# Pattern copies moved from three engines to SP's transfers, with new ranks, load order, gates and places of identity matmuls

## The chip, the cores and the metric

The kernel runs on one core of one Trainium2 chip. The metric is the device time of one execution in microseconds; three executions of the kernel before took 271.74, 271.98 and 272.30 us, the median is 271.98.

## What is computed

Inputs are q, k and v (4 batches, 8 heads, 768 tokens, 64 numbers, float32) and two weight matrices. Attention looks, for each query, only at the 6 best of 24 chunks of 32 keys; the chunks are ranked by an upper bound from each chunk's largest and smallest key. A feed-forward layer follows.

```python
k_min, k_max = k_chunks.min(axis=3), k_chunks.max(axis=3)          # per chunk of 32 keys
ub = sum(maximum(q * k_min, q * k_max))                             # per query and chunk
ub = where(causal, ub, -1e9); top = argsort(ub)[..., -6:]
scores = where(selected & causal, q @ k.T / sqrt(64), -1e9)
x = softmax(scores) @ v                                             # 3072 tokens x 512
h = x @ w_in                                                        # 512 -> 2048
out = (h * clip(h + 3, 0, 6) / 6) @ w_out                           # 2048 -> 512
```

## The kernel before

Two heads make a pair (16 pairs), two pairs with one half of the tokens (384) make a unit (16 units); a batch and a half make a group of the feed-forward layer (8 groups). Units 0 to 3 are batch 0, and they go another way than the rest: their K and Q are turned by TensorE (`turn`, KT and QT in PSUM), while batches 1 to 3 load K and Q in an order that VectorE's 32 by 32 transposes can turn (`load`, `turn_out`, KF and QF).

A unit goes through these steps: the limits of each chunk (`limits`, KMA, VectorE), the bounds (`bounds`, UBT, TensorE; for batches 1 to 3 two units at once), the selection (`bounds_in`, `largest`, `select`, `select_out`, VectorE, ending with the transposed mask MT), the scores (`scores`, SPS, TensorE), exponentials (PT, ScalarE), a triangle (`triangle`, POOL), the values (`values`, PVP, TensorE), and their division (`values_out`, Xb, VectorE). A group then turns its tokens (XTP to XT, or through DRAM as BT, BD, BF) and runs the layer: 16 tiles of HP (4 matmuls each), a relu on ScalarE (U), a multiply on VectorE (GT), and 48 or 64 matmuls of OP, whose sums go out through OT.

The mask enters the scores as further rows of the product: for batch 0 as a matmul with the constant pattern EB, for batches 1 to 3 as rows of K's own tile. K has six tiles (KL0 to KL5), each for the pairs p, p + 6, and so on; the two halves of EB that lie beside a pair's keys are copied into a tile once, before its first pair of batch 1 or later (`beside`, called by `masks_beside`): 12 copies of 64 partitions by 768 bfloat16, each on VectorE, ScalarE or POOL, whichever the planner finds first.

The order of all of this is set by a planner (`Plan`). Each step has an engine or a choice of engines, an estimated length, a rank, the steps that it needs, and the buffers that it takes and gives back. `order` goes through time: whenever an engine is free, the ready step of lowest rank for which there is room begins. The steps are then written out in that order, and every engine runs its own steps in that order, whatever the real times are. `SHIFT` adds a number to the ranks of single steps, found by a search. The planner also has estimates for transfers: `share` is the speed of a transfer of SP beside a transfer of weights.

SP issues nearly all transfers, in its order: first the loads of batch 0 (K, Q and V in `SEQ`), then those of batch 1, and so on. POOL issues the four halves of the weights (WIN and WOUT, two of 1 MB each); ahead of each, `load_weights` reads one number of a tile that must have landed (`GATE`, `seen`): before, the first half of WIN waits for a V load (V2), and each other half for the half before it.

TensorE's clock falls when it idles; so, in the first 45 us, where the planner sees it idle, matmuls with an identity matrix (IDENTB) fill the time. Before, `occupy` puts them behind a step, into 128 columns of its PSUM tile that are left over for this (`spare`).

PSUM has 4 banks for all tiles but the scores (`bank`, m in the plan), which are taken and given back in turn.

Of the kernel before, what the change touches and what calls it, by code (L numbers as in the profile page):

```python
# [45 lines left out]
}  # L46


class Plan:

# [118 lines left out]
def kernel(  # L169
# [188 lines left out]

    spare = []

    def occupy(times):
        for _ in range(times):
# [626 lines left out]
```

## Time and profile before

| | |
|---|---|
| median of three executions | 271.98 us |
| the profiled execution | 271.37 us |
| its span, from the first to the last instruction | 269.7 us |
| TensorE busy | 256.8 us (95%) |
| VectorE, ScalarE, POOL busy | 209.4, 191.6, 128.7 us |
| granted clock | at least 0.99 in each stretch |

Busy times are the sums of an engine's instructions that the profiler recorded. Each engine has a queue of its own and works in its order; a row of a timeline names in brackets for how long the engine had been idle, and which instruction of another engine, or which transfer (DMA), ended the wait. For a transfer the time from issue to landing is told apart from the time in which the issue itself stood in SP's queue.

### The profile page before, as it was taken

The numbers are of one execution on the slowest core, as the hardware profiler recorded it, in microseconds if no ns is written. First come the engines' busy times: TensorE is split into PE (matmuls) and PEld (weight loads), VectorE is DVE, ScalarE is ACT, GpSimd is POOL, SyncE is SP. The second block draws the span as 40 slices with busy tenths as digits, with TensorE's granted clock in tenths as the row PEclk, the third lists the DMA queues.
The fourth block names the chain that finished last, engine by engine and source line by source line (L and its number), as shares of the span: only waits on it lengthen the run. The fifth ranks groups of instructions, "written<-read, shape, count | busy, mean of one in ns | idle before, by whom it ended". The sixth has DMA issues, their size and how long they took to land.

```text
span 269.7 us, 6517 instructions
## 1 busy us (share of the span) xinstructions
PE 256.8 (95%) x2350; PEld 152.7 (57%) x2373; DVE 209.4 (78%) x588; ACT 191.6 (71%) x306; POOL 128.7 (48%) x289
## 2 busy tenths in 40 slices
PE   7997999898999999999999999999999999999994
PEld 4645565654445677644664566654665756555443
DVE  7799898989799997899989999999894424857000
ACT  3589899685527899765984499953998874868021
POOL 4168579533767485559734666752842310200000
PEclk9999999999999999999999999999999999999999
DMA  8999999999948999954995599114103003201122
GB/s 166 219 198 188 190 175 154 176 149 185 212 108 117 127 157 176 186 164 139 150 159 141 157 155 181 40 60 139 39 4 117 5 38 139 58 0 41 39 78 79
DMA packets 122720, 33.71 MB, mean 125 GB/s; under 512 B 113216, under 2 KB 118080, under 8 KB 122688
## 3 DMA queue, kind: packets, MB, share of 16 engines
q1 hardware_dynamic: 117952, 28.71, 62.2%
q0 software_dynamic: 3136, 4.19, 9.5%
q10 hardware_dynamic: 1600, 0.39, 0.7%
q8 instruction: 18, 0.29, 0.6%
q14 instruction: 14, 0.11, 0.2%
HBM read 29.23 MB, written 8.26 MB: 139 GB/s over the span
## 4 chain that ended last, share of the span: by engine, by line
PE 73%; DMA 10%; DVE 8%; SPq 4%; ACT 2%; issue 1%; ACTq 0%; DVEq 0%
PE OP L602 28%; PE HP L587 23%; PE SPS L497 9%; DMA KS<-in_k_dram 8%; PE PVP L530 6%; PE UBT L442 4%; SPq L229 2%; DVE GT L595 2%; PE SPS L494 2%; DMA VS<-in_v_dram 2%; ACT PT L507 1%; PE OP L610 1%; SPq L237 1%; DVE KMA L401 1%; DVE KMA L400 1%
## 5 line engine op out<-in xcount | busy, mean ns | idle before, releaser
L587 PE MATMUL HP<-XT,WIN 128*128 128x384 bf16 x512 | 92.4, 326 | 2.4 <-DVE GT L595 2.3
L507 ACT ACTIVATE PT<-SPS 128x1024 bf16<-128x1024 f32 (+1 forms) x96 | 85.3, 927 | 12.0 <-PE SPS L497 9.9
L602 PE MATMUL OP<-WOUT,GT 128*128 128x512 bf16 x345 | 82.3, 379 | 1.9 <-issue 0.5
L592 ACT ACTIVATE U<-HP,THREE 128x384 bf16<-128x384 f32 x128 | 73.0, 594 | 15.1 <-PE HP L587 8.8
L595 DVE SCALAR_TENSOR_TENSOR GT<-U,HP 128x384 bf16<-128x384 bf16 x128 | 67.2, 545 | 14.9 <-ACT U L592 11.0
L587 PEld LDWEIGHTS <-WIN 128*128 128x128 bf16 x512 | 48.5, 98 | 34.4 <-issue 4.0
L602 PEld LDWEIGHTS <-GT 128*128 128x128 bf16 x368 | 35.1, 98 | 40.2 <-issue 3.7
L512 POOL TENSOR_SCALAR_AFFINE_SELECT PT<-PT 128x256 bf16<-128x256 bf16 x96 | 38.9, 418 | 35.9 <-ACT PT L507 34.9
L497 PE MATMUL SPS<-QLA,KL 128*128 128x384 bf16 (+2 forms) x240 | 36.3, 278 | 0.0
L628 ACT ACTIVATE OT<-OP 128x512 f32<-128x512 f32 x22 | 13.1, 597 | 27.4 <-PE OP L602 27.0
L331 POOL TENSOR_SCALAR_AFFINE_SELECT KL<-KF 64x384 bf16<-64x384 f32 x48 | 23.9, 501 | 14.4 <-DVE KF L387 12.1
L331 POOL TENSOR_SCALAR_AFFINE_SELECT QLA<-QF 64x384 bf16<-64x384 f32 x48 | 24.6, 512 | 12.2 <-DVE QF L387 6.3
L497 PEld LDWEIGHTS <-KL 128*128 128x128 bf16 x240 | 21.7, 98 | 12.8 <-issue 0.6
L530 PEld LDWEIGHTS <-PT 128*128 128x128 bf16 x672 | 23.9, 97 | 3.1 <-issue 0.4
L530 PE MATMUL PVP<-VB,PT 128*128 128x65 bf16 x672 | 25.6, 194 | 0.0
L411 ACT ACTIVATE QR<-QF 128x384 f32<-128x384 f32 x30 | 15.4, 531 | 9.4 <-DVE QF L387 9.3
L542 DVE TENSOR_TENSOR Xb<-PVP,RINV 128x384 bf16<-128x384 f32 x32 | 18.5, 579 | 1.1
L580 POOL COPY XT<-BF 128x384 bf16<-128x384 bf16 x20 | 9.3, 504 | 16.7 <-DMA BF<-BD 16.6
L536 DVE RECIPROCAL RINV<-PVP 128x6 f32<-128x6 f32 x32 | 5.9, 185 | 12.6 <-PE PVP L530 12.2
L387 DVE STREAM_TRANSPOSE KF<-KS 128x384 f32<-128x384 f32 x24 | 13.2, 560 | 1.7 <-DMA KS<-in_k_dram 1.3
L387 DVE STREAM_TRANSPOSE QF<-QS 128x384 f32<-128x384 f32 x24 | 12.8, 555 | 2.0 <-DMA QS<-in_q_dram 2.0
L400 DVE TENSOR_REDUCE KMA<-KF 128x12 f32<-128x384 f32 x24 | 13.1, 545 | 0.4
(80 smaller groups left out, 235.8 us busy)
## 6 DMA issues: line engine op xcount, KB each, us to landing
out_dram<-OT SPq DMA_DIRECT2D x23, 256.0 KB, 2.3
KS<-in_k_dram SPq DMA_DIRECT2D x24, 192.0 KB, 5.5
QS<-in_q_dram SPq DMA_DIRECT2D x24, 192.0 KB, 6.5
VT<-in_v_dram SPq DMA_DIRECT2D x24, 192.0 KB, 4.5
WIN<-in_moe_w_in_dram POOLq DMA_DIRECT2D x2, 1024.0 KB, 9.4
WOUT<-in_moe_w_out_dram POOLq DMA_DIRECT2D x2, 1024.0 KB, 10.1
BD<-BT SPq DMA_DIRECT2D x5, 384.0 KB, 2.4
BF<-BD SPq DMA_DIRECT2D x20, 96.0 KB, 2.3
```

The source lines that it names most:

```text
L331: nc.gpsimd.affine_select(out=to, in_=x, pattern=[[0, n]], compare_op=A.is_ge, fill=0.0, base=0, channel_multiplier=0)
L387: nc.vector.transpose(T[:], st[name][:, st["i"], half * HC:(half + 1) * HC, :].rearrange("p c e -> p (c e)"))
L400: nc.vector.tensor_reduce(out=over, in_=chunks, axis=X_AXIS, op=A.max)
L497: nc.tensor.matmul(SP[:, j, c0:c0 + n], lhsT=KLS[st["pair"] % 6][:, j, jb * P:(jb + 1) * P], rhs=st["QL", half][:, j, at:at + n], start=Tr ...
L507: nc.scalar.activation(PT[:, :, 0:cols], SP[:, :, 0:cols], ACT.Exp, scale=scale)
L512: nc.gpsimd.affine_select(out=PT[:, :, c0:c0 + P], in_=PT[:, :, c0:c0 + P], pattern=[[0, 2], [1, P]], compare_op=A.is_ge, fill=0.0, base=0 ...
L530: nc.tensor.matmul(PVP[:, j, n, :], lhsT=PT[:, j, c0:c0 + P], rhs=st["VB"][:, jb, j, :], start=(jb == 0), stop=(jb == qb))
L542: nc.vector.tensor_tensor(out=to, in0=PVP[:, :, :, 0:D], in1=RINV[:].to_broadcast([P, 2, HB, D]), op=A.mult)
L587: nc.tensor.matmul(HP[:], lhsT=WIN[:, kt, f * P:(f + 1) * P], rhs=g["XT"][:, kt, :, :], start=(kt == 0), stop=(kt == KT_HID - 1))
L592: nc.scalar.activation(U[:], g["HP", f][:], ACT.Relu, bias=THREE[:], scale=1.0)
L595: nc.vector.scalar_tensor_tensor(out=g["GT"][:, f, :], in0=g["U", f][:], scalar=6.0, in1=g["HP", f][:], op0=A.min, op1=A.mult)
L602: nc.tensor.matmul(g["OP", t][:], lhsT=g["GT"][:, f, t * P:(t + 1) * P], rhs=WOUT[:, f, :], start=(f == 0), stop=(f == FT - 1))
```

## The change

- `beside` issues a transfer on SP from EB to K's tile in place of a copy; `masks_beside` plans it as a step of SP and a transfer. 12 copies leave VectorE, ScalarE and POOL, 12 issues come to SP.
- `GATE` reads other tiles: the first half of WIN waits for V1, the second for K4 (the first K load of batch 1), the first half of WOUT reads Q3, the second K1. POOL still issues them one after the other.
- The planner's estimates differ (`BEHIND`, `share` for each kind of transfer, weights 6.3 and 7.3 in place of 6.6 and 7.6), and a transfer under way at 15.3 us takes 1.35 us longer (`FETCH`, a packet of instructions).
- `SHIFT` is another table, so the order differs from the first us to the last; two lines of it are shown.
- Identity matmuls go ahead of a step, into the step's own tile (`occupied`), in steps for which the planner sees TensorE idle over 0.3 us, counted from when their bank came free.

```diff
 SHIFT = {
-    4: -885.8, 6: -49.2, 8: -980.9, 10: -841.2, 12: -1020.7, 14: -50.4, 16: -1.5, 18: -911.2, 20: 8.9, 22: -4.1, 28: -823.6, 30: -2.5, 32: -915.5, 40:
+    10: -869.7, 12: -1031.5, 14: -962.7, 16: -1673.7, 18: -1927.7, 20: -992.4, 22: 73.2, 28: -901.7, 36: 882.4, 38: 1034.2, 40: 956.6, 46: 1047, 52:
...
-    BEHIND = dict(PE=0.24, ACT=0.15, DVE=0.15, POOL=0.15, SP=0.3, DMA=0.9, GEN=0.0, WT=1.2)
+    BEHIND = dict(PE=0.24, ACT=0.15, DVE=0.15, POOL=0.15, SP=0.3, DMA=0.7, GEN=0.0, WT=1.2)
     COLD = 6.5
+    FETCH = 15.3, 1.35
...
+                        st["idle"] = now - max([free[e], *(opened.get((held[0], held[2]), 0.0) for held in st["take"])])
...
-                            length = min(length / 0.15, weights + max(length - 0.15 * weights, 0.0))
+                            length = min(length / st["share"], weights + max(length - st["share"] * weights, 0.0))
+                            if now <= self.FETCH[0] < now + length:
+                                length += self.FETCH[1]
...
+    def occupied(T):
+        for _ in range(idle.pop(0) if idle else 0):
+            nc.tensor.matmul(T[:, 0:P] if len(T.shape) == 2 else T[:, 0, 0, 0:D], lhsT=IDENTB[:], rhs=IDENTB[:, 0:D if len(T.shape) > 2 else P], start=True, stop=True)
+        return T
+
     def bank(name, shape, dtype=FP32):
-        return ps_mix.tile(shape, dtype, name=name, tag=tag("m"))
+        T = ps_mix.tile(shape, dtype, name=name, tag=tag("m"))
+        return occupied(T) if dtype == FP32 else T
...
-    def beside(i, j, e):
-
-        copy(e, KLS[i][OTHER[j], j, :], EB[OTHER[j], i % 2, :])
+    def beside(i, j):
+
+        nc.sync.dma_start(KLS[i][OTHER[j], j, :], EB[OTHER[j], i % 2, :])
...
-    GATE = dict(I0="V2", I1="I0", O0="I1", O1="O0")
+    GATE = dict(I0="V1", I1="K4", O0="Q3", O1="K1")
...
-            made["EB", p % 6] = [add(dict(DVE=0.52, ACT=0.81, POOL=0.85), None, r + RANK["eb"], later(beside, p % 6, j), port=True, after=free.get(("KL", p - 6), []))
-                                 for j in range(2)]
+            made["EB", p % 6] = []
+            for j in range(2):
+                lane = hold("lane")
+                issue = add("SP", 0.42, r + RANK["eb"], later(beside, p % 6, j), after=free.get(("KL", p - 6), []), take=[lane])
+                made["EB", p % 6].append(add("DMA", 0.4, 0, after=[issue], give=[lane], share=0.27))
...
-        there[name, n] = arrive("POOL", 0.95, 6.6 if name == "WIN" else 7.6, (load_weights, name, n, seen), after=got[-1:])
+        there[name, n] = arrive("POOL", 0.95, 6.3 if name == "WIN" else 7.3, (load_weights, name, n, seen), after=got[-1:])
...
+        if step["engine"] == "PE" and step["at"] < 45 and step["idle"] > 0.3 + 0.2 * bool(step["tiles"]):
+            idle[:] = [min(24, int((step["idle"] - 0.1 - 0.2 * bool(step["tiles"])) * 0.8 / 0.058))]
```

Three places show what moves.

**SP, the end of batch 0's loads and the loads of batch 1** (KS and QS are tiles of K and Q; waits on DMAHW are for the eighth transfer before, waits on PE, DVE or Pool for an instruction of that engine). Before:

```order
L237 DMA KS_501<-in_k_dram 32x48x32 [waits DMAHW1_49]
L237 DMA QS_539<-in_q_dram 32x48x32 [waits DMAHW2_49,PE_49]
L237 DMA QS_539<-in_q_dram 32x48x32 [waits DMAHW3_49]
L237 DMA QS_539<-in_q_dram 32x48x32 [waits DMAHW4_49]
L237 DMA QS_539<-in_q_dram 32x48x32 [waits DMAHW5_49]
L237 DMA KS_603<-in_k_dram 32x48x32 [waits DMAHW6_49,PE_49]
```

With the change:

```order
L247 DMA KS_512<-in_k_dram 32x48x32 [waits DMAHW5_49]
L247 DMA QS_568<-in_q_dram 32x48x32 [waits DMAHW6_49,Pool_49]
L247 DMA QS_568<-in_q_dram 32x48x32 [waits DMAHW7_49]
L247 DMA QS_568<-in_q_dram 32x48x32 [waits DMAHW0_49]
L247 DMA QS_603<-in_q_dram 32x48x32 [waits DMAHW1_49,PE_49]
L247 DMA KS_642<-in_k_dram 32x48x32 [waits DMAHW2_49,PE_49,Pool_49]
L247 DMA QS_568<-in_q_dram 32x48x32 [waits DMAHW3_49]
```

A pattern copy now stands ahead of the first K load, three more stand further up among the loads of V, and the first Q load waits for POOL. It goes into the buffer of the Q tile that POOL reads ahead of the first half of WOUT, and the first load of the next K, whose rows follow among those of Q, into that of the K tile read ahead of the second half.

**POOL, the gates of the weights.** Before, the second half of WIN and the first of WOUT:

```order
L313 CAST seenWIN1_786<-WIN_114 1x1
L316 DMA WIN_114<-in_moe_w_in_dram 128x4x1024
...
L313 CAST seenWOUT0_1030<-WIN_114 1x1
L319 DMA WOUT_115<-in_moe_w_out_dram 128x8x512
```

With the change (PT are triangles, KL casts of K, KMA a subtraction of limits):

```order
L323 COPY seenWIN1_858<-KS_512 1x1
L326 DMA WIN_114<-in_moe_w_in_dram 128x4x1024
L341 AFFINE_SELECT KL4_121<-KF_856 64x384 x2
L405 TENSOR_TENSOR KMA_96<-KMA_96 128x12
L513 AFFINE_SELECT PT_823<-PT_823 128x2x128
L513 AFFINE_SELECT PT_881<-PT_881 128x2x128
L513 AFFINE_SELECT PT_891<-PT_891 128x2x128
L341 AFFINE_SELECT KL5_122<-KF_904 64x384 x2
L341 AFFINE_SELECT KL5_122<-KF_919 64x384 x2
L323 COPY seenWOUT0_986<-QS_164 1x1
L329 DMA WOUT_115<-in_moe_w_out_dram 128x8x512
L323 COPY seenWOUT1_1012<-KS_207 1x1
L329 DMA WOUT_115<-in_moe_w_out_dram 128x8x512
```

The read for WOUT's first half (QS_164, the Q of units 1 and 3) stands behind the read of the first K load of batch 1 (KS_512), six casts of K and three triangles.

**VectorE, the multiplies of groups 0 and 1** (GT) and the transposes for batch 1 (KF, QF). Before:

```order
L387 STREAM_TRANSPOSE QF<-QS 128x384
L595 SCALAR_TENSOR_TENSOR GT<-U,HP 128x384
L555 COPY XT<-XTP 128x768
L595 SCALAR_TENSOR_TENSOR GT<-U,HP 128x384
L555 COPY XT<-XTP 128x768
L595 SCALAR_TENSOR_TENSOR GT<-U,HP 128x384 x6
L387 STREAM_TRANSPOSE KF<-KS 128x384
L595 SCALAR_TENSOR_TENSOR GT<-U,HP 128x384 x2
L387 STREAM_TRANSPOSE KF<-KS 128x384
L595 SCALAR_TENSOR_TENSOR GT<-U,HP 128x384
L400 TENSOR_REDUCE KMA<-KF 128x12
```

With the change:

```order
L594 SCALAR_TENSOR_TENSOR GT<-U,HP 128x384 x3
L554 COPY XT<-XTP 128x768
L594 SCALAR_TENSOR_TENSOR GT<-U,HP 128x384
L554 COPY XT<-XTP 128x768
L594 SCALAR_TENSOR_TENSOR GT<-U,HP 128x384 x17
L389 STREAM_TRANSPOSE QF<-QS 128x384
L594 SCALAR_TENSOR_TENSOR GT<-U,HP 128x384 x2
L389 STREAM_TRANSPOSE QF<-QS 128x384
L594 SCALAR_TENSOR_TENSOR GT<-U,HP 128x384 x2
L389 STREAM_TRANSPOSE KF<-KS 128x384
```

Of the 32 multiplies of the two groups, 28 now stand ahead of the first transpose of Q, which the order before puts among them from the fifth on.

## Rows read from the trace of the kernel before

**Rows 1.** Page, part 1: busy us (share of span) x instructions of each engine.

```profile
PE 256.8 (95%) x2350; PEld 152.7 (57%) x2373; DVE 209.4 (78%) x588; ACT 191.6 (71%) x306; POOL 128.7 (48%) x289
```

**Rows 2.** Windows: stretch, length, busy of PE PEld DVE ACT POOL, PEclk, DMA, GB/s.

```profile
45.00:60.00 15.00, 13.42 (x119) 8.35 (x114) 12.69 (x28) 11.89 (x21) 7.34 (x15) 1.00 1.19 153
...
66.00:253.40 187.40, 185.76 (x1647) 109.45 (x1668) 151.93 (x422) 137.69 (x218) 92.13 (x201) 1.00 0.62 109
```

**Rows 3.** Timeline of PE: start, duration, line, op out<-in, count, [idle before <-releaser].

```profile
1.38 2.42 PE L305 MATMUL ZERO<-SELA 128*128 128x384 bf16 x7 [1.38 <-DVE SELA L281]
...
7.27 1.06 PE L365 MATMUL QT<-IDENTB 128*128 128x128 bf16 x16
...
35.61 1.48 PE L587 MATMUL HP<-XT,WIN 128*128 128x384 bf16 x8
...
48.18 1.46 PE L587 MATMUL HP<-XT,WIN 128*128 128x384 bf16 x8 [1.24 <-DVE GT L595]
...
59.31 2.20 PE L587 MATMUL HP<-XT,WIN 128*128 128x384 bf16 x12 [0.29 <-DVE GT L595]
...
62.08 2.85 PE L587 MATMUL HP<-XT,WIN 128*128 128x384 bf16 x16 [0.57 <-DVE GT L595]
...
65.31 2.75 PE L602 MATMUL OP<-WOUT,GT 128*128 128x512 bf16 x11 [0.38 <-DVE GT L595]
...
74.22 4.26 PE L602 MATMUL OP<-WOUT,GT 128*128 128x512 bf16 x19 [0.16 <-issue]
```

**Rows 4.** Timeline of DVE, the same columns.

```profile
7.23 0.55 DVE L255 COPY QF<-QT 128x384 f32<-128x384 f32 x1
...
12.40 0.58 DVE L472 STREAM_TRANSPOSE MT<-SELA 128x384 bf16<-128x384 bf16 x1
...
14.85 0.17 DVE L403 TENSOR_TENSOR KMA<-KMA 128x12 f32<-128x12 f32 x1
...
27.40 0.89 DVE L403 TENSOR_TENSOR KMA<-KMA 128x12 f32<-128x12 f32 x1
...
29.25 0.58 DVE L447 STREAM_TRANSPOSE UB<-UBT 128x384 f32<-128x384 f32 x1 [0.97 <-PE UBT L442]
...
34.40 1.02 DVE L555 COPY XT<-XTP 128x768 bf16<-128x768 bf16 x2
...
35.88 0.58 DVE L387 STREAM_TRANSPOSE KF<-KS 128x384 f32<-128x384 f32 x1 [0.46 <-issue]
...
42.07 0.71 DVE L255 COPY KL<-EB 64x768 bf16<-64x768 bf16 x1
...
47.11 0.58 DVE L387 STREAM_TRANSPOSE QF<-QS 128x384 f32<-128x384 f32 x1 [1.05 <-DMA QS<-in_q_dram]
...
58.24 0.58 DVE L387 STREAM_TRANSPOSE KF<-KS 128x384 f32<-128x384 f32 x1 [0.61 <-DMA KS<-in_k_dram]
...
69.66 0.58 DVE L387 STREAM_TRANSPOSE QF<-QS 128x384 f32<-128x384 f32 x1 [0.55 <-DMA QS<-in_q_dram]
```

**Rows 5.** Timeline of SP's queue: start, time in which the issues stood, count.

```profile
27.98 13.23 SPq L237 DMA_DIRECT2D QS<-in_q_dram  x4
...
83.05 3.59 SPq L237 DMA_DIRECT2D KS<-in_k_dram  x4
```

**Rows 6.** Instructions of tile KL on POOL, ns min, median, max.

```profile
L331 POOL TENSOR_SCALAR_AFFINE_SELECT KL<-KF x48: 495/501/507, 38.1 to 175.6; 64x384 bf16<-64x384 f32 x48
...
L257 POOL TENSOR_SCALAR_AFFINE_SELECT KL<-EB x6: 816/824/947, 3.9 to 49.5; 64x768 bf16<-64x768 bf16 x6
```

**Rows 7.** POOL's timeline; then landing times of KS, and of WIN, to 110 us.

```profile
24.89 1.00 POOL L316 DMA_DIRECT2D WIN<-in_moe_w_in_dram  x1
...
DMA to landing us min/median/max: 2.3/4.7/10.9
...
DMA to landing us min/median/max: 9.1/9.4/9.6
```

**Rows 8.** Timeline of SP's queue: fetches of 96 KB each.

```profile
120.82 1.75 SPq L572 DMA_DIRECT2D BF<-BD  x4
```

More of the change, by code (lines that the diff above doesn't have):

```diff
@@ L61, in __init__, with add @@
         self.lane, self.lanes, self.lean = 0, room["lane"], {}
-    def add(self, engine, length, rank, run=None, after=(), take=(), give=(), port=False, tiles=None, lock=None):
+    def add(self, engine, length, rank, run=None, after=(), take=(), give=(), port=False, tiles=None, lock=None, share=0.2):
         step = dict(lengths=engine if isinstance(engine, dict) else {engine: length}, rank=(rank + SHIFT.get(len(self.steps), 0), len(self.steps)),
-                    run=run, told=isinstance(engine, dict), port=port, tiles=tiles, lock=lock, take=take, give=give, then=[])
+                    run=run, told=isinstance(engine, dict), port=port, tiles=tiles, lock=lock, share=share, take=take, give=give, then=[])
         step["wait"] = {e: len(after) for e in step["lengths"]}
@@ L96, in order @@
         free = {e: busy.get(e, 0.0) for e in self.BEHIND}
-        port, tiles, locks = dict(DVE=0.0, POOL=0.0), None, {}
+        port, tiles, locks, opened = dict(DVE=0.0, POOL=0.0), None, {}, {}
         ready = {e: [] for e in self.BEHIND}
@@ L123, in order @@
                             self.room[held[0]].append(held[2])
+                            opened[held[0], held[2]] = now
             for e, steps in ready.items():
@@ L205, in tag @@
         return f"{kind}{chosen[kind].pop(0)}"
+    idle = [0]
+    def occupied(T):
+        for _ in range(idle.pop(0) if idle else 0):
+            nc.tensor.matmul(T[:, 0:P] if len(T.shape) == 2 else T[:, 0, 0, 0:D], lhsT=IDENTB[:], rhs=IDENTB[:, 0:D if len(T.shape) > 2 else P], start=True, stop=True)
+        return T
     def bank(name, shape, dtype=FP32):
-        return ps_mix.tile(shape, dtype, name=name, tag=tag("m"))
+        T = ps_mix.tile(shape, dtype, name=name, tag=tag("m"))
+        return occupied(T) if dtype == FP32 else T
     src_pool = ctx.enter_context(tc.tile_pool(name="src", bufs=1))
@@ L357 @@
     VS = GT_pool.tile([P, 2, NBLK, 4, D], FP32, name="VS", tag=tag("gt"))
-    spare = []
-    def occupy(times):
-        for _ in range(times):
-            nc.tensor.matmul(spare[-1], lhsT=IDENTB[:], rhs=IDENTB[:, 0:spare[-1].shape[-1]], start=True, stop=True)
     def turn(st, name, half):
@@ L370, in turn @@
             x = st[name][:, half, :, st["own"], :]
-            T = bank(name[0] + "T", [P, HS + P])
-            spare.append(T[:, HS:])
-            T = st[name, half] = T[:, 0:HS]
+            T = st[name, half] = bank(name[0] + "T", [P, HS])
             for t in range(HB):
@@ L431, in bounds @@
         for u in us:
-            T = bank("UBT", [P, HS + P])
-            spare.append(T[:, HS:])
-            u["UBT"] = T[:, 0:HS]
+            u["UBT"] = bank("UBT", [P, HS])
             u["joint"] = len(us) > 1
@@ L486, in scores @@
         SP = st["SP", half, t] = ps_score.tile([P, 2, 512], FP32, name="SPS", tag=tag("s"))
+        occupied(SP[:, 0, :])
         for jb, q0, n, c0 in PLAN[half][t]:
@@ L521, in values @@
             X_tiles[st["b"], half] = xpool.tile([P, HB, DMODEL], BF16, name="Xb", tag=tag("x"))
-        T = bank("PVP", [P, HS + P])
-        spare.append(T[:, 2 * HB * (D + 1):])
-        PVP = st["PVP", half] = T[:, 0:2 * HB * (D + 1)].rearrange("p (j n d) -> p j n d", j=2, n=HB)
+        PVP = st["PVP", half] = bank("PVP", [P, 2, HB, D + 1])
         for j in range(2):
@@ L667, in arrive @@
                 issued.append(got)
-                got = add("GEN", 1.2, 0, after=[got])
-            landed.append(add("WT" if engine == "POOL" else "DMA", length, 0, after=[got], give=lane))
+                got = add("GEN", 1.0, 0, after=[got])
+            landed.append(add("WT" if engine == "POOL" else "DMA", length, 0, after=[got], give=lane, share=0.1 if length > 1 else 0.15))
         return landed
@@ L908 @@
             kept = add("SP", 0.37, -3000, later(keep_words, g), after=before, take=[held_bd, lane])
-            kept, m = add("DMA", 1.4, 0, after=[kept], give=[held_bt, lane]), []
+            kept, m = add("DMA", 1.4, 0, after=[kept], give=[held_bt, lane], share=0.45), []
             for part in range(4):
@@ L939 @@
                     a = add("SP", 0.37, -2000, later(result_last_store, g, t, part), after=[a], take=[lane])
-                    add("DMA", 0.6, 0, after=[a], give=[ot, lane])
+                    add("DMA", 0.6, 0, after=[a], give=[ot, lane], share=0.4)
                 continue
@@ L948 @@
             a = add("SP", 0.37, -2000, later(result_out, g, t, nc.sync), after=[a], take=[lane])
-            add("DMA", 0.75, 0, after=[a], give=[ot, lane])
+            add("DMA", 0.75, 0, after=[a], give=[ot, lane], share=0.4)
         r += RANK["step"]
-    for step in (steps := plan.order(PE=3.7, ACT=4.25, DVE=4.4, POOL=3.2, SP=3.7, DMA=1.6, WT=1.6)):
+    for step in plan.order(PE=3.7, ACT=4.25, DVE=4.4, POOL=3.2, SP=3.7, DMA=1.6, WT=1.6):
         chosen = {}
@@ L954 @@
             chosen.setdefault(kind, []).append(number)
-        spare.clear()
+        idle[:] = []
+        if step["engine"] == "PE" and step["at"] < 45 and step["idle"] > 0.3 + 0.2 * bool(step["tiles"]):
+            idle[:] = [min(24, int((step["idle"] - 0.1 - 0.2 * bool(step["tiles"])) * 0.8 / 0.058))]
         if step["run"]:
             step["run"](*[step["engine"]] if step["told"] else [])
-        if spare:
-            end = step["at"] + step["length"]
-            idle = min(other["at"] for other in steps if other["engine"] == "PE" and other["at"] > step["at"]) - end
-            if end < 45 and idle > 0.25:
-                occupy(min(16, int((idle - 0.2) * 0.8 / 0.058)))
 _INS = ['q', 'k', 'v', 'moe_w_in', 'moe_w_out']
```

31 rows, old and new, of the table SHIFT are left out of this document.

## The prediction

> **What bounds the kernel now.** I read the page first: TensorE is busy 95% of the span, VectorE 78% [rows 1]. Next the busy time by stretch: from 66 to 253.4 us TensorE is idle 1.64 us in 187.4, so a gain there is at most that [rows 2]. What can still be won lies before 66 us. The timeline of TensorE shows where: the first HP matmul starts at 35.61, and after it TensorE stops four times, for 1.24, 0.29, 0.57 and 0.38 us, 2.48 in all; the first OP matmul comes at 65.31 [rows 3]. All four stops end with a GT multiply of VectorE, and the timeline of VectorE says why they were late [rows 4]: at 47.11 a transpose of Q had waited 1.05 us for its load, at 58.24 one of K 0.61, and the GT multiplies stand behind these in VectorE's queue. So the stops are late loads of batch 1, passed on through VectorE's order. SP's own timeline shows the loads blocked at their issue: four take 13.23 us beside the weights and 3.59 us at 83 us, when the weights are done [rows 5]. The granted clock is 1.00 in both stretches [rows 2]; it limits nothing.
>
> The sum is made in the profiled execution: span 269.7, its own time 271.37; the median 271.98 is 0.61 above that. All terms are differences, added to the median.
>
> **The path to the first HP.** VectorE sets it: from its first MT transpose (12.40) to the XT copies (34.40) there are 22.0 us, in which it waited 0.97 us for UBT, and a subtraction (KMA) took 0.89 us where others take about 0.17: 1.7 us of waiting [rows 4]. The changed order does in that stretch one cast of V less (some 0.55) and three KMA subtractions of 0.1 less, and four steps of Q tiles more (a copy of 0.55, as at 7.23, and three smaller ones, 1.4 together by my estimate): 0.5 us more work [rows 4]. It also gives both Q tiles of the first selection to ScalarE, one after the other, where each engine did one: some 0.45 us later at the start (an estimate from the Q copy at 7.23). If all waits go: 1.7 - 0.5 - 0.45 = 0.7 us earlier. **Term: -0.7**, between +0.5 (the waits stay) and -1.2 (the start is no later). The first half of WIN, issued at 24.89 and at least 9.1 us under way, forbids more: 34.0 [rows 7].
>
> **The four stops.** The changed VectorE order has 17 GT multiplies in a row, and the first transpose of Q stands behind 28 of 32; so no load waits among them, and the 2.48 us go. In their place comes the first K load. Four pattern copies now stand ahead of it on SP; the nearest row, the BF fetches of 96 KB, has four issues in 1.75 us [rows 8], so the load begins 1.8 us later and its first transpose, at 35.88 before, comes at 37.7. VectorE would have been ready at 34.7 and has nothing else queued ahead. The first GT stands behind that transpose and two reductions (1.5 us): 39.2. HP, PVP and XTP share four PSUM banks; with two tiles of HP, one PVP and another HP tile held, I count some 1.0 us in which TensorE waits for a bank (0 to 2). **Term: -2.48 + 1.0.**
>
> **The second half of WIN** is gated by that K load: issue at about 38.7 instead of 34.53. With the longest duration beside loads, 9.6, it lands at 48.3 [rows 7]. The first matmul that needs it is the 33rd of HP, which began at 48.18 before [rows 3]; it now stands one PVP (0.9 us) later in the order, less 0.7 and 1.24, plus 1.0: 48.1. **Term: +0.2** (0 to 1.5). The Trainium skill ("DMA: Bandwidth & Descriptors", section Bandwidth) has 1 MB in 6.15 us with nothing beside it, and SP is held back just then; by that estimate it lands at 44.9 and the term is 0. No row here shows a weight alone.
>
> **The gates of WOUT, and what queues behind them.** This is the edit that I weigh most. The dummy read that gates the first half of WOUT now reads the Q tile of units 1 and 3, and the second K of unit 1. The new loads of batch 1 go into these very buffers, so SP's first Q load waits for a POOL instruction (the order shows the wait), and POOL reaches it only after the first K load, two casts, three triangles and four more casts of K. The last transposes for these end at about 41.4, four casts of 0.50 follow [rows 6]: about 43, where these loads began at 27.98 [rows 5]. SP issues in order: 12 loads wait with it. The last is due before the first bounds of batch 1 (UBT), which in TensorE's new order stand behind 40 OP matmuls. Before, OP began at 65.31 with 12 HP (1.95 us) still to come [rows 3], so at 67.3 by the new order, less 0.7, less 2.48, plus 1.0 and 0.2: 65.3, and 40 x 0.2165 later, 73.9 (19 OP in 4.26, of which the first is longer [rows 3]). The loads: first landing 4.5 us after issue (4.7 is the median of the K loads [rows 7]), 47.5; then a load each 2.8 us beside the weights (12 landed between 35.88 and 69.66 [rows 4]), until WOUT's second half is in at about 66: seven or eight. The other four or five go at 0.9 to 1.3 us [rows 5]: 71. Two transposes and a relu: 72.5, in time by 1.4 us. The sixth load completes the first Q and is due at 62.8; it lands at 61.5. **Term: +0.3.** The low end is 0. The high end: at 3.47 us each (41.6 us for the 12 before, issue to landing) and never faster, the last lands at 85.7, and UBT waits 13 us; I take the low side because the row at 83 us shows the pace without weights.
>
> **The copies of patterns.** Twelve copies leave the engines: six on POOL (0.82 each [rows 6]), three on ScalarE, three on VectorE (up to 0.71, at 42.07 [rows 4]). Those after 30 us run, most of them, beside a TensorE that has no stop between 35.61 and 46.9 [rows 3], so I cost them at nothing; if that cover is gone, the two that ScalarE does there are worth 1.6 us, at POOL's duration. The eight copies behind the loads cost SP 3.5 us at about 70 us, ahead of values that the first PVP of batch 1 needs after 83 us: nothing.
>
> **Identity matmuls.** 49 instead of 42, now ahead of a step and in its own tile. 16 take 1.06 us [rows 3], 0.056 each; they fill waits, unless a wait is shorter than planned: 15 stand ahead of the last turns of K, 0.85 us at most. **Term: +0.2** (0 to 0.85).
>
> **Everything after 66 us** has a new order too. 1.64 us of idle time can go, and as much may come: **+0.2** (-1.0 to +1.5).
>
> Sum: -0.7 - 2.48 + 1.0 + 0.2 + 0.3 + 0.2 + 0.2 = -1.28. 271.98 - 1.28 = **270.7 us**. A change of 0.2% (0.54 us) is about what a measurement can tell from none.
>
> **The rivals.**
> - *It goes as drawn* (0.15): no bank waits behind the first K load, the first HP 1.2 us earlier, WIN in time: -1.2 - 2.48 = -3.7, 268.3 us. For it: the 1.7 us of waiting in VectorE's chain, and the copies that leave the engines around 30 to 50 us. Against it: the K load is later on SP in any case.
> - *Given back at once* (0.17): the first K load lands 2 us late and the waits in the chain stay: terms of 0 instead of -0.7 and +1.8 instead of +1.0, the rest as above, +0.2 in all: 272.2 us, no change. For it: SP blocks at its issues [rows 5]; against it: the waits in the chain have other causes than K.
> - *The loads behind the gate come late* (0.22): TensorE stands before the first UBT, or VectorE before the sixth load. Without its term of 0.3 the sum is 270.4. It decides from a last landing at 74.5 on, 3.5 us later than worked out above: then UBT starts at 76.0, 2.1 us late, and the time passes 272.5. If the last 4.4 loads go at half of the free pace, 2.2 us each from 66 on, the last lands at 75.6: +3.2, **273.6 us**, slower. For it: SP's row at 13.23 us for four. Against it: the free pace at 83 us [rows 5]. At 2.8 us each to the end, 78.3, it would be 276.3.
> - *A stop long enough for the clock* (0.06): the longest stop in this trace is 1.24 us, and the granted clock in its stretch is 1.00 [rows 2, 3]. A stop of 3 us or more before UBT would be a new thing here. At the start, seven matmuls of 384 columns take 2.42 us, 0.32 each, where eight HP take 1.46 or 0.16 each [rows 3]: the lower of the two levels would double the OP and UBT that follow, for 3 us more, 275 us. The Trainium skill ("TensorE: Matmul & The Clock Gate", Part 1) says that a gate halves the clock after an idle time. The durations at the start agree with it; the granted clock of the rows shows no fall.
>
> The forecast itself has 0.40. **Chances:** faster 0.40 + 0.15 = 0.55, same 0.17, slower 0.22 + 0.06 = 0.28. **Range:** 267.8 to 274.0; it takes in the first three cases and most of the slower one (the bound of 13 us is left out, with most of the clock's case: some 0.12), and 0.05 below. The forecast's own range is 269.4 to 271.5.
>
> **What would show it.** Right: first HP at 34.5 to 35.5; one or two stops between 38 and 42 that end with a GT; none from 50 to 65; SP's first Q load of batch 1 at about 43 behind POOL; the last transposes of Q just before the first UBT at about 74; OP starting near 65. Wrong: SP not held (then the wait costs nothing and the K load decides); a wait of VectorE for Q or K among or right after the GT multiplies at 60 to 75; a TensorE stop of over 2 us before UBT; the first HP later than 35.6; a granted clock under 0.95 in a stretch.

## The result, and the profile after

The changed kernel took 275.22 us in the median (274.56 to 276.81, four executions), the kernel before 271.86 in the same session: a ratio of 1.0102 (95% interval 1.0059 to 1.0144), so 1.0% slower and clear of the noise, where 270.7 us was forecast. The profiled execution took 274.66 us, its span is 273.0 (before 271.37 and 269.7): 3.3 us more. TensorE is busy 258.3 us in place of 256.8 and idle 14.7 in place of 12.9: 1.5 us more of busy time and 1.8 us more of stops.

TensorE's timeline, changed kernel (columns as in [rows 3]):

```profile
35.73 0.82 PE L586 MATMUL HP<-XT,WIN 128*128 128x384 bf16 x4
...
41.49 1.22 PE L529 MATMUL PVP<-VB,PT 128*128 128x65 bf16 x27 [0.56 <-POOL PT L513]
...
47.21 1.21 PE L529 MATMUL PVP<-VB,PT 128*128 128x65 bf16 x27 [0.19 <-POOL PT L513]
...
50.98 13.81 PE L586 MATMUL HP<-XT,WIN 128*128 128x384 bf16 x84
66.99 8.79 PE L601 MATMUL OP<-WOUT,GT 128*128 128x512 bf16 x39 [2.20 <-DVE GT L594]
75.72 0.88 PE L442 MATMUL UBT<-QF,KMA 64*32 64x384 f32 x16
...
84.78 0.82 PE L498 MATMUL SPS<-QLA,KL 128*128 128x384 bf16 x6
...
97.22 0.60 PE L498 MATMUL SPS<-QLA,KL 128*128 128x256 bf16 x4 [0.56 <-ACT PT L508]
...
99.01 0.60 PE L498 MATMUL SPS<-QLA,KL 128*128 128x384 bf16 x4 [0.39 <-ACT PT L508]
```

The four stops of [rows 3] are gone; 84 HP run without a break from 50.98 on. One stop of 2.20 us before the first OP has taken their place. It ends with a GT multiply, and VectorE's timeline says why that was late (compare [rows 4]):

```profile
38.04 0.58 DVE L389 STREAM_TRANSPOSE KF<-KS 128x384 f32<-128x384 f32 x1 [2.79 <-DMA KS<-in_k_dram]
...
65.92 0.58 DVE L389 STREAM_TRANSPOSE QF<-QS 128x384 f32<-128x384 f32 x1 [2.52 <-DMA QS<-in_q_dram]
...
74.67 1.03 DVE L389 STREAM_TRANSPOSE QF<-QS 128x384 f32<-128x384 f32 x2
```

The first transpose of Q waits 2.52 us for its load, with the GT behind it. SP's queue, and POOL's timeline around the gates ([rows 5, 7] are their counterparts):

```profile
24.36 10.69 SPq L247 DMA_DIRECT2D KS<-in_k_dram  x4
44.18 14.85 SPq L247 DMA_DIRECT2D QS<-in_q_dram  x4
59.15 1.64 SPq L247 DMA_DIRECT2D KS<-in_k_dram  x1
```

```profile
38.03 0.18 POOL L323 COPY seenWIN<-KS 1x1 f32<-1x1 f32 x1 [2.42 <-DMA KS<-in_k_dram]
38.50 0.78 POOL L326 DMA_DIRECT2D WIN<-in_moe_w_in_dram  x1 [0.28 <-issue]
...
43.98 0.17 POOL L323 COPY seenWOUT<-QS 1x1 f32<-1x1 f32 x1
44.10 0.93 POOL L329 DMA_DIRECT2D WOUT<-in_moe_w_out_dram  x1
```

SP has issued its first four K loads by 35.05 and then issues nothing until 44.18: the first Q load goes 0.03 us after POOL's read of the old tile has ended. What this leaves undone shows in the transfer engines' strip, 40 slices of 36 to 44 us, busy tenths; the kernel before:

```profile
DMA  9999999999999989999999999999999999999999
```

and the changed kernel:

```profile
DMA  9999510000000000000196692689999999999999
```

For 13 slices, 2.6 us, nothing is moved at all, at a time in which the kernel before had all engines full. Twelve loads of K and Q follow. The first of them landed at 53.27, the sixth, which completes the first Q, at 65.84, the last at 74.09. The first score of batch 1 comes at 84.78 us, where it was at 79.86; how much of this is the hold and how much the new order, e1 below will tell. Two further losses lie behind it. From 80 to 100 us TensorE is busy for less; before and after, the windows (stretch, length, busy of PE, PEld, DVE, ACT, POOL, clock, DMA, GB/s):

```profile
80.00:100.00 20.00, 19.84 (x197) 12.78 (x199) 18.78 (x71) 16.48 (x22) 13.27 (x33) 1.00 1.13 128
```

```profile
80.00:100.00 20.00, 18.46 (x175) 10.44 (x176) 16.26 (x69) 15.65 (x21) 13.12 (x27) 1.00 0.96 167
```

And a UBT of the next group drips out with the transposes of a late Q: 1.45 us from its start to the next OP before, 2.94 after.

```profile
119.58 0.88 PE L442 MATMUL UBT<-QF,KMA 64*32 64x384 f32 x16
120.25 0.85 PE L442 MATMUL UBT<-QR,KMA 64*32 64x384 f32 x16
121.03 6.22 PE L602 MATMUL OP<-WOUT,GT 128*128 128x512 bf16 x27
```

```profile
124.70 1.42 PE L442 MATMUL UBT<-QF,KMA 64*32 64x384 f32 x14
...
125.96 1.51 PE L442 MATMUL UBT<-QR,KMA 64*32 64x384 f32 x12
127.64 3.62 PE L601 MATMUL OP<-WOUT,GT 128*128 128x512 bf16 x16 [0.16 <-issue]
```

The orders differ, so equal times do not mean equal progress. To compare, I take at a matmul its start less the work ahead of it in TensorE's order, each matmul at its duration in a full stretch (HP 0.163 us, OP 0.217, PVP 0.031; an estimate from rows such as the 84 HP above). What is left is all the time lost so far:

| time lost up to | before | changed | e1 (below) |
|---|---|---|---|
| the first OP | 23.95 | 23.67 | 21.96 |
| the first score of batch 1 | 25.34 | 25.05 | 23.35 |
| the scores at about 105 us | 25.48 | 27.57 | 26.33 |
| the scores at about 130 us | 26.63 | 29.54 | 27.37 |
| the last OP group | 28.96 | 31.95 | 29.80 |

In spite of the 2.20 us the changed kernel is 0.3 us ahead at the first OP. It then loses more than the kernel before does: 2.4 us between the first score and 105, 0.8 up to 130, and 0.1 after.

### The profile page after: what moved, and what is told of

It reads as the page before. It is cut to its first block, busy times and chain, and to the rows that moved or that the text cites. A ratio compares the mean times of both kernels' runs of the same rounds, so it can differ in the third digit from the quotient of the medians.

```text
span 273.0 us, 6533 instructions
## 1 busy us (share of the span) xinstructions
PE 258.3 (95%) x2363; PEld 153.1 (56%) x2380; DVE 204.1 (75%) x582; ACT 189.0 (69%) x306; POOL 125.0 (46%) x283
## 4 chain that ended last, share of the span: by engine, by line
PE 70%; DMA 10%; POOL 6%; SPq 4%; DVE 4%; issue 2%; ACT 2%; ACTq 1%; POOLq 0%; DVEq 0%
PE HP L586 26%; PE OP L601 22%; PE SPS L498 9%; PE PVP L529 6%; DMA KS<-in_k_dram 5%; SPq L247 3%; PE UBT L442 3%; POOL QLA L341 2%; DMA VT<-in_v_dram 2%; DMA VS<-in_v_dram 1%; POOL KL L341 1%; DMA QS<-in_q_dram 1%; ACT PT L508 1%; PE OP L609 1%; POOL PT L513 1%
## 5 line engine op out<-in xcount | busy, mean ns | idle before, releaser
L508 ACT ACTIVATE PT<-SPS 128x1024 bf16<-128x1024 f32 (+2 forms) x96 | 86.5, 942 | 10.4 <-PE SPS L498 7.6
L586 PE MATMUL HP<-XT,WIN 128*128 128x384 bf16 x512 | 90.5, 326 | 0.0
L627 ACT ACTIVATE OT<-OP 128x512 f32<-128x512 f32 x21 | 12.5, 596 | 27.9 <-PE OP L601 22.2
L529 PE MATMUL PVP<-VB,PT 128*128 128x65 bf16 x672 | 26.6, 194 | 1.2 <-POOL PT L513 1.1
L413 ACT ACTIVATE QR<-QF 128x384 f32<-128x384 f32 x29 | 14.7, 550 | 14.6 <-DVE QF L389 10.6
L579 POOL COPY XT<-BF 128x384 bf16<-128x384 bf16 x20 | 9.4, 514 | 21.7 <-DMA BF<-BD 21.7
L267 POOL TENSOR_SCALAR_AFFINE_SELECT VB<-VT 128x768 bf16<-128x768 f32 x12 | 10.9, 909 | 7.0 <-DMA VT<-in_v_dram 6.7
```

What stands on the lines that cost most here:

```text
L413: nc.scalar.activation(QR[:], QF[:], ACT.Relu)
L508: nc.scalar.activation(PT[:, :, 0:cols], SP[:, :, 0:cols], ACT.Exp, scale=scale)
L529: nc.tensor.matmul(PVP[:, j, n, :], lhsT=PT[:, j, c0:c0 + P], rhs=st["VB"][:, jb, j, :], start=(jb == 0), stop=(jb == qb))
L586: nc.tensor.matmul(HP[:], lhsT=WIN[:, kt, f * P:(f + 1) * P], rhs=g["XT"][:, kt, :, :], start=(kt == 0), stop=(kt == KT_HID - 1))
```

## Is it the hold, the order, or the transfers?

Theory A: the read for WOUT's gate holds SP's first Q load, and what follows is late. Rival B: the new order loses the time by itself. Rival C: SP's eight late pattern transfers (5.2 us of its queue) delay the loads behind them.

**e1: the gates of WOUT read a constant.** Same orders on all engines; SP's Q and K loads no longer wait for POOL's reads. Both of WOUT's reads change, but only the first had held SP: the second, of the K tile, ended at 45.20, and the K load that waits for it had its turn in SP's queue at 59.15.

```diff
-        nc.gpsimd.tensor_copy(seen[:], seen_in())
+        nc.gpsimd.tensor_copy(seen[:], THREE[0:1, 0:1] if name == "WOUT" else seen_in())
```

> The changed kernel, in which the two instructions that gate WOUT's halves read the constant THREE in place of the Q and K tiles; order and planner as they are. POOL reaches them at the same places (43.98 and 45.03 us), but SP's first Q load of batch 1 no longer waits for POOL's reading. Theory A (the held Q load makes everything that follows late): the load goes at about 35.1 instead of 44.18 us, the 2.20 us stop before the first OP goes, the first score of batch 1 comes at 79 to 81 instead of 84.78 us, the waits for ACT's PT around 97 and the slow UBT at 124.70 go as well: 270.5 to 272.5 us. Rival B (the order after 66 us loses the time by itself, it uses up OP before the scores come): only the stop goes and is given back, 274 to 275.3 us. Rival C (SP's eight pattern transfers at 72.95 to 80.12 us make the V, K and Q loads behind them late): 274 to 275. A rival on the other side: the Q loads now run beside the second half of WIN, which lands after 48.3 us, and HP stops for it near 48 us by 1 to 4 us: 275 to 278.

Measured: ratio to the kernel before 0.9992 (0.9960 to 1.0024), 272.94 us where before took 272.94 on that chip. The strip of 36 to 44 us has no hole left, the Q load goes at 32.96, and the stop before OP is gone:

```profile
DMA  8853599999699999769999999966799999989999
```

```profile
65.28 8.80 PE L601 MATMUL OP<-WOUT,GT 128*128 128x512 bf16 x40
...
94.78 0.60 PE L498 MATMUL SPS<-QLA,KL 128*128 128x256 bf16 x4 [0.56 <-ACT PT L508]
...
96.57 0.60 PE L498 MATMUL SPS<-QLA,KL 128*128 128x384 bf16 x4 [0.39 <-ACT PT L508]
...
98.72 0.51 PE L550 MATMUL XTP<-IDENTB,Xb 128*128 128x128 bf16 x6 [1.22 <-DVE Xb L541]
```

The next group's UBT takes 1.79 us instead of 2.94. The whole loss against the kernel before is gone with these reads. But theory A expected the waits at 97 us to go too and the first score by 81 us; it comes at 83.08, and the stretch up to 105 us still loses 3.0 us (23.35 to 26.33), where the kernel before loses 0.1. That part is not the hold's; it is what rival B expected of the order. The table shows what is the hold's, changed kernel less e1: 1.7 us at the first OP, still 1.7 at the first score, 1.2 at 105, and 2.2 at 130 and at the end. So it is the one stop before OP, and some 0.9 us around the late UBT of the next group.

**e2: the eight late patterns on POOL and ACT.**

```diff
-        nc.sync.dma_start(KLS[i][OTHER[j], j, :], EB[OTHER[j], i % 2, :])
+        hands.append(("SP", "POOL", "ACT")[(len(hands) >= 4) * (1 + j)])
+        if hands[-1] == "SP":
+            nc.sync.dma_start(KLS[i][OTHER[j], j, :], EB[OTHER[j], i % 2, :])
+        else:
+            copy(hands[-1], KLS[i][OTHER[j], j, :], EB[OTHER[j], i % 2, :])
```

> The changed kernel with the eight later pattern copies (those that SP issues from 72.95 us on) written by POOL (4) and ACT (4) instead of by SP's transfers, at the same places of the order; the first four stay with SP. SP loses 8 issues there, about 5.2 us of its queue, and POOL and ACT gain 4 copies of about 0.82 us each between 66 and 82 us. Theory A: the loads are late by the hold, the copies lie on engines that wait anyway or push UBT's successors by up to 1: 274.5 to 276.5 us. Rival C: the VT loads come 3 to 5 us earlier, the second set of K and Q loads too (K at 85 instead of 89.78 us, Q of the next group by 112 instead of 118), the slow UBT at 124.70 goes: 272 to 273.7 us. Rival B: 275, as the changed kernel.

Measured: 1.0131 (1.0088 to 1.0173), no better than the changed kernel. Rival C falls.

**e3: no identity matmuls** (`idle` stays empty).

> The changed kernel without the 49 identity matmuls in the steps' own tiles; nothing else. All three theories: the granted clock stays 1.00 and the time is that of the changed kernel, 274.8 to 275.7 us. If the identity matmuls delay the transposes behind them: 274.2 to 274.7. If they hold the clock: the granted clock falls below 1.00 in the first 45 us and the time is over 276.

Measured: 1.0122 (1.0040 to 1.0204), as the changed kernel; the granted clock is 1.00 in every stretch from the start to 67 us without them, so the third expectation falls: no trace here shows that they hold the clock. The interval is too wide for the half microsecond between the first two expectations.

**h1: the changed kernel with the ranks of the kernel before.**

> The changed kernel (its gates, pattern transfers, identity matmuls and planner costs) with the 212 rank shifts of the kernel before, carried over step by step. Rival B: the order after 66 us was the loss, so 271.5 to 273.5 us. Theory A: the Q load is held as before this edit and the loads stay late, 274 to 277 us. Rival C: 274 to 276 us. If ranks are only good together with the costs they were searched with: over 276.

Measured: 1.109 (1.104 to 1.114), 302.19 us, with stops of up to 7.35 us. That is the last of the four expectations: these ranks were searched with other costs, and do not carry over. So the run says nothing on B.

**m1: the hold put into the kernel before.** One line; the order of no engine changes.

```diff
+        seen = landing["Q2"][1] if what == "O0" else seen
```

> The kernel before, in which POOL's gate of WOUT's first half (at 45.42 us) reads the Q tile that SP's first Q load of batch 1 overwrites, in place of WIN; nothing else. SP's queue then stands from 27.98 to about 45.6 us with 16 loads behind it. Theory A: the same loss as in the changed kernel, larger by the longer hold (17.6 us instead of 9.1): 3 to 9 us over the kernel before, with a stop of PE before or among the first OP and the first score of batch 1 after 83 us. Rival B (the loss lies in the order after 66 us, not in the hold): within 1 us of the kernel before.

Measured: 1.0502 (1.0458 to 1.0545), 13.3 us slower, more than I expected. SP's first Q load, and the stop of TensorE that follows:

```profile
45.32 10.21 SPq L237 DMA_DIRECT2D QS<-in_q_dram  x4
```

```profile
60.09 2.72 PE L587 MATMUL HP<-XT,WIN 128*128 128x384 bf16 x8 [13.45 <-DVE GT L595]
```

Held 17.3 us longer than in [rows 5], the load stops TensorE for 13.45 us, again through a GT behind a transpose of Q. (8 HP behind it take 2.72 us, 1.46 in [rows 3], so part of the 13.3 us is a lower clock.) That the hold costs time is shown from both sides: the reads taken from the changed kernel give back all it had lost, and one put into the other costs 13.3 us.

## The clock

**a2: the changed kernel once more.**

> The changed kernel as it is, beside the other three on one chip. 0.8 to 1.3% over the kernel before. Where its profile shows a stop of 2.2 us before the first OP, the granted clock stays at 1.00; where the stop is 2.7 us or more, as in e2 and e3, the clock shows 0.50 for about 3.5 us behind it and the time is 1.3 to 2 us longer than where it is 2.2.

Measured: 1.0099 (1.0068 to 1.0129), median 276.37; nine executions, four at 274.83 to 275.60 and five at 276.37 to 276.97. The profile is of one at 276.58. There the stop before OP is 2.82 us instead of 2.20, and the granted clock behind it is at its lower level (1.2 GHz of 2.4) for most of 67 to 71 us; the second window is of the first profile of the changed kernel, behind its stop of 2.20:

```profile
67.73 10.33 PE L601 MATMUL OP<-WOUT,GT 128*128 128x512 bf16 x40 [2.82 <-DVE GT L594]
```

```profile
67.00:71.00 4.00, 3.27 (x9) 1.14 (x9) 2.53 (x6) 1.91 (x4) 2.00 (x4) 0.57 1.00 125
```

```profile
67.00:71.00 4.00, 3.95 (x18) 1.85 (x19) 2.69 (x6) 1.45 (x4) 1.88 (x5) 1.00 1.09 145
```

40 OP take 10.33 us instead of 8.8 (e1). 1.5 us of slower OP and 0.6 of longer stop cover the 1.9 us between the two profiles of one kernel. The same shows in e2 and e3 (stops of 2.76 and 2.80). So the rival on the clock, which I had put behind a stop of 3 us or more, came true in these three profiles. It does not follow every such stop: in e5 (below) one of 2.81 us leaves the clock at 1.00. Whether it makes the two groups of times is open: the mean granted clock on record for each execution does not part them (0.991 to 1.000 in the four shorter ones, 0.993 to 0.998 in the five longer).

## What is left: 94 to 105 us

With the hold gone, why is e1 not faster than before, with 2.0 us in hand at the first OP? Each of these runs changes e1 in one place.

**e5: SP's K loads ahead of three stores** that stood before them.

```diff
+    steps = steps[:stores[2]] + early + [st for st in steps[stores[2]:] if not any(st is x for x in early)]
```

> The kernel of e1 (WOUT's gates read a constant), with SP's four K loads of batch 1's second half moved ahead of the three stores of results that stood before them (in e1 SP stands 7.12 us at these stores from 80.90 on, and the K loads go at 88.08). Theory A2 (what is left of the loss in e1, 2.7 us between 94 and 99, comes from loads that SP issues late: DVE waits 2.36 us for K at 97.41, and the work on X stands behind it in DVE's order): K lands before 92, the 1.22 us stop of XTP goes, 1.0 to 1.6 us less than e1, so 0.3 to 0.6% under the kernel before. Rival B2 (PE has no dense work left there and waits for ACT's PT whatever DVE does): within 0.5 us of e1. Rival on the other side: the stores come late, the two result tiles hold the banks of OP, 0.5 to 2 us more than e1.

Measured: 1.0085 (1.0051 to 1.0119), by the ratios 2.5 us over e1. The XTP stop did go, but ScalarE now waits for the stores' result tile, and a stop of 2.81 us for its PT is the price. The granted clock behind it is 1.00:

```profile
91.79 0.60 ACT L627 ACTIVATE OT<-OP 128x512 f32<-128x512 f32 x1 [3.30 <-DMA out_dram<-OT]
```

```profile
92.92 0.38 PE L498 MATMUL SPS<-QLA,KL 128*128 128x256 bf16 x2 [2.81 <-ACT PT L508]
```

```profile
92.90:96.90 4.00, 3.98 (x35) 2.44 (x35) 1.45 (x4) 3.21 (x5) 2.70 (x7) 1.00 1.05 210
```

**e7: WOUT's second half after the first has landed**, behind POOL's work at 49 us.

```diff
+    steps = [x for n, st in enumerate(steps) for x in ([st, second] if n == last else [] if st is second else [st])]
```

> The kernel of e1 with the second half of WOUT issued behind POOL's last work before its idle stretch (about 49 us) and gated on the landing of the first half (about 53 us), where e1 has both halves outstanding from 45.2 on and each takes 14.0 us to land. Theory A3 (two outstanding weight loads slow the K and Q loads beside them, K 13.4 us to landing in e1): K and Q of batch 1 land 1 to 2 us earlier, UBT comes at 72.5 to 73.5 instead of 74.01 us, the first score at 81.5 to 82.5, 0.5 to 1.2 us less than e1. Rival: the transfers share the same bandwidth until 66 us whatever their order, within 0.4 us of e1. Rival on the other side: WOUT's second half lands after 67 us and the first OP stop for it, 0.5 to 2 us more than e1.

Measured: 0.9991 (0.9966 to 1.0017), as e1. The last of the twelve loads of K and Q landed at 71.55 (70.56 in e1), UBT came at 74.44 and the first score at 83.50, no earlier than in e1: A3 falls, and the loads behave as the rival of a shared bandwidth has it. The time alone could not rule out A3's smallest gain of 0.5 us.

**e8: both.**

> Both edits (K loads ahead of the stores, second half of WOUT behind the first) on the kernel of e1. If A2 and A3 both hold, the gains add: 1.5 to 2.8 us less than e1, 0.5 to 1.0% under the kernel before. If only one holds, that one's figure; if neither, e1.

Measured: 1.0152 (1.0104 to 1.0201). A stop of 3.36 us for PT, by e5's wait, and a lower clock behind it (0.61 over 95 to 100 us).

**e9, e10: two OP pieces kept for the stops**, on e1 and on e7.

```diff
+            for name, args in (("result", (1, 2)), ("result", (1, 3)), ("result_scale", (1,)), ("result_out", (1,)))]
```

> The kernel of e1 (WOUT's gates read a constant) with the last two OP pieces of the first group (4 matmuls of 512 columns each, 0.87 us of PE each) kept back: one ahead of the scores that wait for ACT at 94.78 us, one ahead of the XTP that waits for DVE at 98.72; the result's scaling and store go with them. Theory B2 (in 94 to 99 us PE has used up its dense work, and what waits for PT and Xb is not covered): the three stops of 0.56, 0.39 and 1.22 us shrink to under 0.8 in sum, 0.8 to 1.7 us less than e1, 0.3 to 0.7% under the kernel before. Rival A2 (late K loads hold DVE, and PE with it, whatever PE has in hand): the stops move, within 0.5 us of e1. Rival on the other side: the bank that these pieces keep longer holds PVP or XTP, 0.3 to 1.5 us more than e1.

> The same two pieces kept back, on the kernel of e7 (WOUT's second half issued after the first has landed), which stood 0.1 us under e1. If B2 holds 0.8 to 1.7 us less than e7; if the earlier K and Q of e7 have already taken part of the XTP stop (0.46 there instead of 1.22 us), 0.5 to 1.2 us.

Measured: 0.9993 (0.9971 to 1.0015) and 1.0016 (0.9980 to 1.0051). In e9 the stops moved forward (0.59 at 92.29, 0.68 at 94.06, 0.39 at 97.41, 0.69 at 99.89; 2.35 us in sum, 2.17 in e1): OP was needed as cover where it had been, too. B2 as I put it falls.

**e15: ACT's two result copies to DVE.**

```diff
+        if getattr(st["run"], "what", "") == "result_scale" and st["engine"] == "ACT" and 84 < st["at"] < 95:
+            st["engine"] = "DVE"
```

> The kernel of e1 with the two result copies that ACT does in 84 to 95 us (0.59 us each, at 87.07 and 93.22) done by DVE at the same places of the order. Theory D (from the first score at 83.08 on, ACT's PT set the pace and PE, with OP used up, waits for them at 94.78, 96.57): ACT's part gets 1.2 us shorter, the two stops for PT fall from 0.95 to under 0.4 us, 0.6 to 1.2 us less than e1. Rival A2 (the stretch is set by DVE and the late K load, 1.22 us stop of XTP): the stops move to XTP, within 0.4 us of e1. Rival on the other side: DVE's copies push MT or Xb by 0.7 each, 0.3 to 1 us more than e1.

Measured: 1.0030 (0.9999 to 1.0060). The stops for PT stayed (0.47, 0.39), the one of XTP grew to 2.13: theory D falls. DVE stood 2.96 us before the transpose of K.

**e12, e13, e16: the late patterns on POOL and ACT**, on e1, on e7, and on e7 with e15's edit.

> The kernel of e1 with the eight later pattern copies on POOL and ACT (as in e2). In e2 that edit moved the time by +0.8 us at most against the changed kernel, with Q still late. Rival C in its last form (SP's 5.2 us of pattern issues cost once Q is no longer held): 0.8 to 2 us less than e1. Theory A: DVE and PE wait for the stores and K loads, which stand behind the results and not behind the patterns: within 0.6 us of e1; and up to 1.5 more where ACT's four copies push QR and QLA.

> The kernel of e7 (WOUT's gates read constants or WOUT, second half issued behind the first) with the eight later pattern copies on POOL and ACT. If the small gains of e7 and e12 are real and add: 0.3 to 0.5% under the kernel before. If they are noise: that of e1, 0.1% under it.

> e13 with the two result copies on DVE as in e15. If theory D holds: 0.6 to 1.2 us less than e13, 0.4 to 0.9% under the kernel before; otherwise as e13.

Measured: 0.9979 (0.9952 to 1.0006), 0.9973 (0.9943 to 1.0002), 1.0007 (0.9982 to 1.0032). None can be told from the kernel before; e13 is the lowest of all.

**e17, e18, e19: work taken out from behind the late K.** e17 (on e1) and e18 (on e13) move DVE's Xb ahead of the transpose of K, e19 also POOL's PT ahead of K's cast.

```diff
+    late = next(st for st in steps if what(st, "values_out", 0) == 7)
+    at = next(n for n, st in enumerate(steps) if what(st, "turn", "KS", 0) == 9 and st["engine"] == "DVE")
+    steps = steps[:at] + [late] + [st for st in steps[at:] if st is not late]
```

> The kernel of e1 with one exchange in DVE's order: RINV and Xb of the last of the four PVP (at 97.91 and 98.11 us) stand ahead of the transpose of K that waits 2.36 us for its load at 97.41. No other engine's order changes. Theory A2 (DVE's wait for the late K load, with work for PE behind it, is what is left of the loss): Xb goes at 96 to 96.5, the 1.22 us stop of XTP goes, 0.9 to 1.6 us less than e1, so 0.2 to 0.6% under the kernel before. Rival: PE then stops at the next thing behind the same K load (XT, for the first HP of the next group at about 101), within 0.4 us of e1.

> The same exchange on the kernel of e13 (WOUT's second half behind the first, eight pattern copies on POOL and ACT), whose XTP stop is 1.43 us. Theory A2: 1.0 to 1.7 us less than e13, 0.5 to 0.9% under the kernel before. Rival: within 0.4 us of e13, 0.2 to 0.4% under the kernel before.

> The kernel of e18 with one more exchange, in POOL's order: the last PT of the PVP that stops PE for 1.24 us at 100.01 stands ahead of the cast of KL, which waits 2.13 us for K's transpose. Theory A2 (what is left of the loss is work that stands behind the late K load on DVE and POOL): both the XTP stop and the PVP stop are gone, PE loses under 1.4 us between 94 and 104 instead of 2.5, 0.8 to 1.4 us less than e18, 0.3 to 0.6% under the kernel before. Rival: PE stops for XT before the next HP, or for ACT's PT, within 0.4 us of e18.

Measured: 1.0008 (0.9982 to 1.0034), 0.9997 (0.9975 to 1.0019), 1.0022 (1.0000 to 1.0044). Each stop that was removed had another behind it. In e18 XTP no longer stops; PVP does, since POOL's cast of K waited for the same transpose:

```profile
98.41 1.07 POOL L341 TENSOR_SCALAR_AFFINE_SELECT KL<-KF 64x384 bf16<-64x384 f32 x2 [2.13 <-DVE KF L395]
99.55 0.41 POOL L519 TENSOR_SCALAR_AFFINE_SELECT PT<-PT 128x256 bf16<-128x256 bf16 x1
```

```profile
100.01 0.85 PE L535 MATMUL PVP<-VB,PT 128*128 128x65 bf16 x22 [1.24 <-POOL PT L519]
```

In e19 that went, and HP stopped 0.56 us for XT at 100.42; the time lost between the first score and 105 us is 2.7 us (23.69 to 26.41). So I leave open what sets these 2.5 to 3 us. Shown is that it comes with the new order, without the hold (e1), and that moving the K load, the OP, the copies or three rows behind the load did not remove it; that the late K load has a part in it is argued, not shown. No version here can be told to beat the kernel before.

## Why the prediction was wrong, point by point

- **The path to the first HP, -0.7:** did not come; 35.73 for 35.61. VectorE's stretch from the first MT to the XT copies began earlier, at 11.69 instead of 12.40, but took 22.5 us instead of 22.0: the wait for UBT went, and one of 1.00 for PVP and one of 0.52 for XTP came. The XT copies came 0.17 us earlier, at 34.23. The bound I gave, WIN at 34.0, used the shortest landing of [rows 7] and the old issue. WIN went at 25.35, 0.46 us later, and its first half took 10.0 us, to 35.33. In e1 and e3 HP waits for WIN itself (0.35 and 0.27 us).
- **The four stops, -2.48 + 1.0:** the four stops went, and K's first transpose came at 38.04 (37.7 forecast). The 1.0 was near for another reason: 0.75 us of stops for PVP, which end with POOL's PT and not at a bank. That size was luck.
- **WIN's second half, +0.2:** right in size, no stop. It was issued at 38.50 and landed at 47.95, 9.46 us later, as the rows had it (48.3). The Trainium skill's figure ("DMA: Bandwidth & Descriptors", Bandwidth) gave 44.9 in the prediction; it is the busy time of the transfer engines alone, and I had counted it from the issue. m1 has the row that was missing, a weight half by itself: issued at 34.26, landed 8.23 us later, with data moving for some 5.8 us of that (36.2 to 42.0 in the strip of 36 to 44 us), near the 6.15 of the Trainium skill:

```profile
DMA  0296489999999999999999999999510000000000
```

- **The gates of WOUT, +0.3: the step that failed.** The mechanism was right to 1.2 us: SP held until 44.18 (43 forecast). The size was not. I let the first load land 4.5 us after its issue and the rest follow at 2.8 us each, the pace of the kernel before, in which the weights came one half after the other. Now both halves were outstanding at once (10.9 and 15.4 us to landing): the first load took 9.1 us, the next two 15.6 and 16.0, and the first four stood 14.85 us in SP's queue. So the sixth load, due at 62.8 and forecast for 61.5, landed at 65.84, and the first Q was transposed at 65.92: VectorE waited 2.52 us and TensorE 2.20. In m1, where loads of the same size begin beside one half, the first four stood 10.21 us and the sixth landed 16.6 us after the first issue instead of 21.7; that the second half makes the difference is read from these two kernels and not tested by itself. Even the slow pace that I had set aside for the high end, 3.47 us each, would have put the sixth at 64.9 and shown the stop. I worked that pace out for the last load alone. Twelfth, it landed at 74.09 (71 forecast), and TensorE did not stop for UBT. e1 puts the term at 2.2 us by the profiles (274.66 to 272.50, clock at 1.00 in both) and at 3.0 by the ratios (1.0102 to 0.9992), whose intervals allow some 1.5 either way.
- **Identity matmuls, copies: +0.2 and 0:** no run shows more (e2, e3, e12), though e3 could not show half a microsecond.
- **Everything after 66 us, +0.2 (-1.0 to +1.5):** too small. e1 has no hold, was 2.0 us ahead at the first OP, and ends 0.8 behind: about 2.8 us, most of it between 94 and 105. The bound of 1.64 us of idle time [rows 2] bounds what can be won there, not what can be lost, and I had used it for both.
- **The rivals:** the outcome is the third, the loads behind the gate come late, at 0.22. It named the wait that came, VectorE before the sixth load, but priced another, TensorE before UBT, which needed a last landing at 74.5 and did not occur. That its 273.6 to 276.3 us took in the measured time was luck. The one on the clock came true in some profiles; its 3 us stood in no row, and a2 shows 1.5 us of slower OP.

## What to carry to other kernels

A dummy read is a reader like any other: before a gate is placed, look for what next overwrites the tile that it reads, and count all that is queued behind that write; here one number read 9 us late left the transfer engines empty for 2.6 us. A planner that knows the edge from landing to issue, but not the edge from the read to the next load into the buffer, will place that load too early and never see the cost. And where the likeliest harm is lateness, try the slow pace on every date that is due, the nearest first: here the sixth load had 1.3 us in hand and came 4.3 us later than forecast, while the last load, by which I had decided, made no stop.

## What the hardware showed that I had not expected

A stop of 2.20 us before OP left the granted clock at 1.00, and one of 2.82 us at the same place was followed by 0.50 (a2, 67.5 to 70 us): 0.6 us more of waiting went with 1.9 us more of time. But the length of the last stop does not decide alone. In e15 a stop of 2.13 us, with two shorter ones in the 5 us before it, was followed by a lower clock as well (0.75 over 100 to 105 us), and in e5 one of 2.81 us was not (1.00 over 92.9 to 96.9 us). What decides stays open here. The Trainium skill ("TensorE: Matmul & The Clock Gate", Part 1) has the clock halved after idle time; a2, e2, e3 and e15 agree, and e5 shows a stop after which it was not.
